# Transposing V by crossbar DMA instead of on TensorE in a two-block attention backward kernel

## The chip, the cores and the metric

The kernel runs on one core of one Trainium2 chip. The metric is the device time of one execution in microseconds (us). Engines are named as in the profile: PE (TensorE matmul), PEld (TensorE weight load), DVE (VectorE), ACT (ScalarE), POOL (GpSimd), SP (SyncE, which issues most transfers).

## The reference

Two independent attention blocks A and B, forward and all gradients. Each has 8 batches of 96 queries, 32 heads of width 128, 512 cached keys and values per head and batch, and a model width of 640.

```python
def _A_ref(x, k_cache, v_cache, wq, wo):          # B is the same
    q = (x @ wq) -> [B, H, Sq, Dh]
    scores = einsum("bhqd,bhkd->bhqk", q, k_cache) * Dh ** -0.5
    p = softmax(scores)
    o = einsum("bhqk,bhkd->bhqd", p, v_cache)
    return o -> [B, Sq, H*Dh] @ wo
# outputs: concat(a, b) and the gradients of x, k_cache, v_cache, wq, wo of both blocks
```

The backward pass needs dP = dO · Vᵀ, so V is used in both orientations: as stored (keys on partitions) for the output, and transposed (Dh on partitions) for dP. K is used transposed for the scores and as stored for dQ.

## The kernel before

The kernel is a software pipeline over 512 (head, batch) pairs. One pair enters per "tick"; its stages s1 to s8 run in the ticks after it, so that each tick holds one stage of each of several pairs, plus "filler" work per head (projections, weight gradients) that is spread over the eight ticks of a head.

```python
OFF = dict(ld=0, s1=2, s2=3, s3=3, s4=4, s5=5, s6=6, s7=7, s8=8)   # tick of each stage

def bank(shape, dt, name):            # all PSUM tiles share 8 banks
    return ps.tile(shape, dt, name=name, tag="bank")

def c_ld(h, b):                       # loads, one batch per transfer
    K_sb = kvp.tile([128, KC, 128], BF16, name="K_sb", bufs=11)
    V_sb = kvp.tile([128, KC, 128], BF16, name="V_sb", bufs=8)
    nc.sync.dma_start(K_sb[:], kc[b, h]...)
    nc.sync.dma_start(V_sb[:], vc[b, h]...)

def c_s1(h, b):                       # K and V transposed on PE, one eviction on DVE
    kvT_ps = bank([128, 2 * Sk], BF16, "kvT_ps")
    for c in range(KC):
        nc.tensor.transpose(kvT_ps[:, c*128:(c+1)*128], st["K_sb"][:, c, :], ident[:])
    for c in range(KC):
        nc.tensor.transpose(kvT_ps[:, Sk + c*128: ...], st["V_sb"][:, c, :], ident[:])
    KVT = wk.tile([128, 2 * Sk], BF16, name="KVT", bufs=5)
    nc.vector.tensor_copy(KVT[:], kvT_ps[:])

def c_s2a(h, b):                      # scores on PE, minus their maximum on DVE
    S_ps = bank([Sq, Sk], F32, "S_ps")
    nc.tensor.matmul(S_ps[:], QT_h[:, tok], KT)
    nc.vector.tensor_reduce(negm[:], S_ps[:], axis=AX.X, op=ALU.max, negate=True)

def c_s2b(h, b):                      # exp on ACT: reads S_ps for the last time
    nc.scalar.activation(E_sb[:], S_ps[:], ACT.Exp, bias=negm[:], accum_out=rowsum[:])

def c_s6(h, b):                       # dP and the row term, then dS on DVE
    nc.tensor.matmul(dP_ps[:], dOT_h[:, tok], VT)
    nc.tensor.matmul(dl_ps[:], prod[:], ones[:, 0:1])
    nc.vector.scalar_tensor_tensor(dS_sb[:], dP_ps[:], dl_ps[:, 0:1], P_sb[:], ...)
# ... (s3 to s5, s7, s8, the fillers and the set-up are cut)
```

## Time and profile before

| | before |
|---|---|
| time, median of 3 (lowest to highest) | 1850.45 us (1850.15 to 1851.11) |
| PE, DVE, ACT, POOL busy | 98%, 82%, 78%, 42% |
| chain that ended last | PE 95% |
| DMA, SyncE queue and GpSimd queue | 46.2% and 10.7% of the 16 engines |

The engine line of the page of before (busy us, share of the span, instructions), its chain of waits and its two busy DMA queues:

```profile
PE 1818.4 (98%) x26595; PEld 1571.4 (85%) x26744; DVE 1518.6 (82%) x3309; ACT 1434.4 (78%) x4041; POOL 777.9 (42%) x1378
...
q1 hardware_dynamic: 296480, 270.53, 46.2%
q0 software_dynamic: 19872, 60.32, 10.7%
...
PE 95%; POOL 2%; issue 1%; DVE 1%; DMA 1%; ACT 0%; POOLq 0%; SPq 0%; ACTq 0%
```

PE is the limit: 95% of the chain is PE, and the next engine, DVE, is busy for 82% (PEld is the loading of weights for PE itself).

The timeline of PE before (start, duration of the group, engine, line, operation):

```profile
1000.65 0.39 PE L243 MATMUL kvT_ps<-ident,K_sb 128*128 128x128 bf16 x4
1000.87 0.39 PE L245 MATMUL kvT_ps<-ident,V_sb 128*128 128x128 bf16 x4
1001.09 0.33 PE L370 MATMUL dq_dst_ps<-dST_sb,K_sb 128*128 128x96 bf16 x4
```

The group of four V transposes is on record as 0.39 us long, but the next group starts 0.22 us after it: matmuls overlap, and what one costs is the distance to the start of the next, about 56 ns here.

The same stretch by engine, in the windows view (busy us of PE, PEld, DVE, ACT, POOL; granted clock; DMA share; GB/s):

```profile
1000.00:1025.00 25.00, 24.89 (x382) 21.36 (x381) 22.10 (x49) 21.98 (x65) 11.46 (x22) 1.00 0.65 201
```

The timeline of before around one batch's scores, all engines, other lines left out:

```profile
1002.99 0.38 PE L259 MATMUL S_ps<-KVT,QT_h 128*96 128x512 bf16 x1
...
1003.45 0.68 DVE L159 COPY Qnat_h<-n_ps 96x1024 bf16<-96x1024 bf16 x1
1004.04 0.68 DVE L261 TENSOR_REDUCE negm<-S_ps 96x1 f32<-96x512 f32 x1
...
1004.81 0.68 ACT L271 ACTIVATE E_sb<-S_ps,negm 96x512 bf16<-96x512 f32 x1 [0.98 <-DVE negm L261]
1005.40 0.19 ACT L271 ACTIVATION_READ_ACCUMULATOR E_sb<-S_ps,negm 96x1 f32 x1
...
1005.62 0.16 PE L354 MATMUL dl_ps<-ones,prod 128*96 128x1 bf16 x1
1005.65 0.22 PE L445 MATMUL dwq_ps<-dQnat,x_nat 128*128 128x128 bf16 x1
```

The maximum (negm) runs on DVE after a 0.68 us copy that is in line before it; exp on ACT waits for it and is through 2.6 us after the scores began. The filler matmul at 1005.65 follows dl_ps without a gap.

### The profile page before, as it was taken

Reading aid. Unit: us, or ns where it says so; the run is one execution under the profiler, and the core shown is the slowest. Engines: PE = TensorE matmul, PEld = TensorE weight load, DVE = VectorE, ACT = ScalarE, POOL = GpSimd, SP = SyncE. Lnnn points to the kernel's source line nnn. Section 1 sums busy time; section 2 is a strip of 40 time slices with the busy share of each in tenths; the row PEclk is TensorE's granted clock in tenths of the full one; section 3 lists DMA queues with packets and bytes.
Section 4 is the critical chain, followed back from the end, with each engine's and each line's share of the span. In section 5 each row is a group of like instructions: output and inputs, shape, how many; then the busy total and the mean of one; then the engine's idle time right before and its main releaser. Section 6 shows DMA issues by size and latency. Waiting matters only on the chain.

```text
span 1848.8 us, 69797 instructions
## 1 busy us (share of the span) xinstructions
PE 1818.4 (98%) x26595; PEld 1571.4 (85%) x26744; DVE 1518.6 (82%) x3309; ACT 1434.4 (78%) x4041; POOL 777.9 (42%) x1378
## 2 busy tenths in 40 slices
PE   6999999999999999999999999999999999999998
PEld 5888888888888888888888888888888888888887
DVE  5888867888788887888878887678887888878885
ACT  4888877888668886788767888788876788767882
POOL 4444433444334443345455444334433444333435
PEclk9999999999999999999999999999999999999999
DMA  7666654666546655566575665456655566555652
GB/s 229 196 193 202 192 162 149 199 195 193 164 148 194 201 183 165 159 191 205 186 229 173 196 194 184 160 167 198 192 175 164 171 196 199 159 165 176 201 168 84
DMA packets 316688, 335.32 MB, mean 181 GB/s; under 512 B 38368, under 2 KB 302048, under 8 KB 316352
## 3 DMA queue, kind: packets, MB, share of 16 engines
q1 hardware_dynamic: 296480, 270.53, 46.2%
q0 software_dynamic: 19872, 60.32, 10.7%
q8 instruction: 210, 3.44, 0.8%
q14 instruction: 126, 1.03, 0.2%
HBM read 171.57 MB, written 159.12 MB: 179 GB/s over the span
## 4 chain that ended last, share of the span: by engine, by line
PE 95%; POOL 2%; issue 1%; DVE 1%; DMA 1%; ACT 0%; POOLq 0%; SPq 0%; ACTq 0%
PE q_ps L210 11%; PE o_ps L480 10%; PE dV_ps L330 6%; PE kvT_ps L243 6%; PE kvT_ps L245 6%; PE dK_ps L394 6%; PE dP_ps L352 6%; PE S_ps L259 6%; PE dwq_ps L445 6%; PE dwo_ps L425 5%; PE optp_ps L313 5%; PE dq_dst_ps L377 5%; PE optp_ps L306 5%; PE dq_dst_ps L370 5%; PE n_ps L225 3%; PE nat_ps L410 2%
## 5 line engine op out<-in xcount | busy, mean ns | idle before, releaser
L290 POOL TENSOR_SCALAR P_sb<-E_sb,rinv 96x512 bf16<-96x512 bf16 x512 | 354.2, 692 | 780.5 <-DVE rinv L281 775.2
L271 ACT ACTIVATE E_sb<-S_ps,negm 96x512 bf16<-96x512 f32 x512 | 349.1, 682 | 291.2 <-DVE negm L261 288.1
L356 DVE SCALAR_TENSOR_TENSOR dS_sb<-dP_ps,dl_ps,P_sb 96x512 bf16<-96x512 f32 x512 | 383.3, 749 | 108.1 <-PE dl_ps L354 103.1
L247 DVE COPY KVT<-kvT_ps 128x1024 bf16<-128x1024 bf16 x512 | 350.0, 684 | 70.7 <-PE kvT_ps L245 69.0
L261 DVE TENSOR_REDUCE negm<-S_ps 96x1 f32<-96x512 f32 x512 | 347.6, 679 | 35.8 <-PE S_ps L259 30.1
L332 ACT ACTIVATE dV_sb<-dV_ps 128x512 bf16<-128x512 f32 x512 | 313.3, 612 | 0.0
L396 ACT ACTIVATE dK_sb<-dK_ps 128x512 bf16<-128x512 f32 x512 | 300.5, 587 | 15.7 <-PE dK_ps L394 12.9
L319 ACT ACTIVATE PT_sb<-optp_ps 128x384 bf16<-128x384 bf16 x512 | 253.4, 495 | 0.0
L245 PE MATMUL kvT_ps<-ident,V_sb 128*128 128x128 bf16 x2048 | 198.0, 219 | 0.0
L394 PE MATMUL dK_ps<-Qnat_h,dS_sb 96*128 96x128 bf16 x2048 | 197.9, 219 | 0.0
L243 PE MATMUL kvT_ps<-ident,K_sb 128*128 128x128 bf16 x2048 | 197.9, 219 | 0.0
L330 PE MATMUL dV_ps<-dOnat_h,P_sb 96*128 96x128 bf16 x2048 | 197.9, 219 | 0.0
L259 PE MATMUL S_ps<-KVT,QT_h 128*96 128x512 bf16 x512 | 193.8, 379 | 2.2 <-DVE KVT L247 1.9
L352 PE MATMUL dP_ps<-KVT,dOT_h 128*96 128x512 bf16 x512 | 195.2, 381 | 0.0
L342 POOL TENSOR_TENSOR prod<-OT_h,dOT_h 128x96 bf16<-128x96 bf16 x512 | 186.2, 364 | 19.4 <-ACT OT_h L316 14.4
L243 PEld LDWEIGHTS <-K_sb 128*128 128x128 bf16 x2048 | 147.3, 98 | 36.9 <-issue 1.9
L379 DVE COPY dST_sb<-dq_dst_ps 128x384 bf16<-128x384 bf16 x512 | 175.4, 343 | 1.8 <-PE dq_dst_ps L377 0.8
L313 PE MATMUL optp_ps<-ident,P_sb 96*128 96x96 bf16 x2048 | 171.6, 205 | 2.3 <-POOL P_sb L290 2.0
L377 PE MATMUL dq_dst_ps<-ident,dS_sb 96*128 96x96 bf16 x2048 | 172.1, 206 | 0.5 <-DVE dS_sb L356 0.4
L306 PE MATMUL optp_ps<-PT_sb,V_sb 128*128 128x96 bf16 x2048 | 172.1, 206 | 0.0
L370 PE MATMUL dq_dst_ps<-dST_sb,K_sb 128*128 128x96 bf16 x2048 | 170.7, 206 | 0.0
L445 PE MATMUL dwq_ps<-dQnat,x_nat 128*128 128x128 bf16 x1920 | 143.2, 219 | 0.0
(84 smaller groups left out, 3949.8 us busy)
## 6 DMA issues: line engine op xcount, KB each, us to landing
out_dram<-dV_sb SPq DMA_DIRECT2D x512, 128.0 KB, 2.0
out_dram<-dK_sb SPq DMA_DIRECT2D x512, 128.0 KB, 2.3
K_sb<-in_A_k_cache_dram SPq DMA_DIRECT2D x256, 128.0 KB, 2.4
V_sb<-in_A_v_cache_dram SPq DMA_DIRECT2D x256, 128.0 KB, 2.5
K_sb<-in_B_k_cache_dram SPq DMA_DIRECT2D x256, 128.0 KB, 2.4
V_sb<-in_B_v_cache_dram SPq DMA_DIRECT2D x256, 128.0 KB, 2.5
out_dram<-dwq_sb POOLq DMA_DIRECT2D x64, 160.0 KB, 3.0
out_dram<-dwo_sb POOLq DMA_DIRECT2D x64, 160.0 KB, 2.7
```

The costliest lines, as they stand in the source:

```text
L243: nc.tensor.transpose(kvT_ps[:, c * 128:(c + 1) * 128], st["K_sb"][:, c, :], ident[:])
L245: nc.tensor.transpose(kvT_ps[:, Sk + c * 128:Sk + (c + 1) * 128], st["V_sb"][:, c, :], ident[:])
L247: nc.vector.tensor_copy(KVT[:], kvT_ps[:])
L259: nc.tensor.matmul(S_ps[:], hs["QT_h"][:, tok], st["KT"], start=True, stop=True)
L261: nc.vector.tensor_reduce(negm[:], S_ps[:], axis=AX.X, op=ALU.max, negate=True)
L271: nc.scalar.activation(E_sb[:], st["S_ps"][:], ACT.Exp, bias=st["negm"][:], scale=1.0, accum_out=rowsum[:])
L290: nc.gpsimd.tensor_scalar(P_sb[:], st["E_sb"][:], st["rinv"][:], 0.0, op0=ALU.mult, op1=ALU.add)
L330: nc.tensor.matmul(dV_ps[:, c * 128:(c + 1) * 128], P_sb[:, c * 128:(c + 1) * 128], hs["dOnat_h"][:, b * 128:(b + 1) * 128], start=True, s ...
L332: nc.scalar.activation(dV_sb[:], dV_ps[:], ACT.Identity, scale=1.0)
L352: nc.tensor.matmul(dP_ps[:], hs["dOT_h"][:, tok], st["VT"], start=True, stop=True)
L356: nc.vector.scalar_tensor_tensor(dS_sb[:], dP_ps[:], dl_ps[:, 0:1], st["P_sb"][:], op0=ALU.subtract, op1=ALU.mult)
L394: nc.tensor.matmul(dK_ps[:, c * 128:(c + 1) * 128], dS_sb[:, c * 128:(c + 1) * 128], hs["Qnat_h"][:, b * 128:(b + 1) * 128], start=True, s ...
```

## The change

The intent: PE has no time to spare and DMA has, so the four V transposes per pair leave PE, and a crossbar transfer from SBUF to SBUF makes VT. DVE then evicts half as many columns. Loads and crossbar transfers handle two batches each, to halve their number.

```diff
-OFF = dict(ld=0, s1=2, ...)
+OFF = dict(ld=-1, vt=1, s1=2, ...)
     def c_ld(h, b):
-            K_sb = kvp.tile([128, KC, 128], BF16, name="K_sb", bufs=11)
-            V_sb = kvp.tile([128, KC, 128], BF16, name="V_sb", bufs=8)
-            nc.sync.dma_start(K_sb[:], kc[b, h]...)
-            nc.sync.dma_start(V_sb[:], vc[b, h]...)
+            K_sb = kvp.tile([128, 2, KC, 128], BF16, name="K_sb", bufs=7)
+            V_sb = kvp.tile([128, 2, KC, 128], BF16, name="V_sb", bufs=5)
+            nc.sync.dma_start(V_sb[:], vc[b:b + 2, h]...)
+            nc.sync.dma_start(K_sb[:], kc[b:b + 2, h]...)
+    def c_vt(h, b):
+            VT = kvp.tile([128, 2 * KC, 128], BF16, name="VT", bufs=4)
+            nc.sync.dma_start_transpose(VT[:], V_sb[:].rearrange("p a c d -> p (a c d)"))
     def c_s1(h, b):
-            kvT_ps = bank([128, 2 * Sk], BF16, "kvT_ps")
+            kT_ps = bank([128, Sk], BF16, "kT_ps")
             # four transposes of K, as before
-            # four transposes of V
-            KVT = wk.tile([128, 2 * Sk], BF16, name="KVT", bufs=5)
-            nc.vector.tensor_copy(KVT[:], kvT_ps[:])
+            KT = wk.tile([128, Sk], BF16, name="KT", bufs=3)
+            nc.vector.tensor_copy(KT[:], kT_ps[:])
# ... c_ld and c_vt are called for even b only
```

More of the change, by code (lines that the diff above doesn't have):

```diff
@@ L43 @@
 SL_SETUP = 96
-OFF = dict(ld=0, s1=2, s2=3, s3=3, s4=4, s5=5, s6=6, s7=7, s8=8)
+OFF = dict(ld=-1, vt=1, s1=2, s2=3, s3=3, s4=4, s5=5, s6=6, s7=7, s8=8)
 HK = dict(pA=-5, pB=-3, pC0=[-2, 0], pC1=[-1, 0], pD1=1, pD0=2, qA0=13, qA1=17, qB=[20, 17], qD=[(18, 0, 2), (19, 2, 5)])
@@ L230, in f @@
         def f():
-            K_sb = kvp.tile([128, KC, 128], BF16, name="K_sb", bufs=11)
-            V_sb = kvp.tile([128, KC, 128], BF16, name="V_sb", bufs=8)
-            nc.sync.dma_start(K_sb[:], kc[b, h].rearrange("(p c) d -> p c d", c=KC))
-            nc.sync.dma_start(V_sb[:], vc[b, h].rearrange("(p c) d -> p c d", c=KC))
-            CS[(blk, h, b)] = dict(K_sb=K_sb, V_sb=V_sb)
+            K_sb = kvp.tile([128, 2, KC, 128], BF16, name="K_sb", bufs=7)
+            V_sb = kvp.tile([128, 2, KC, 128], BF16, name="V_sb", bufs=5)
+            nc.sync.dma_start(V_sb[:], vc[b:b + 2, h].rearrange("b (p c) d -> p b c d", c=KC))
+            nc.sync.dma_start(K_sb[:], kc[b:b + 2, h].rearrange("b (p c) d -> p b c d", c=KC))
+            for i in range(2):
+                CS[(blk, h, b + i)] = dict(K_sb=K_sb[:, i], V_sb=V_sb[:, i], V2=V_sb)
+        return f
+    def c_vt(h, b):
+        def f():
+            VT = kvp.tile([128, 2 * KC, 128], BF16, name="VT", bufs=4)
+            nc.sync.dma_start_transpose(VT[:], CS[(blk, h, b)]["V2"][:].rearrange("p a c d -> p (a c d)"))
+            for i in range(2):
+                CS[(blk, h, b + i)]["VT"] = VT[:, i * KC:(i + 1) * KC].rearrange("p c k -> p (c k)")
         return f
@@ L240, in f @@
             st = CS[(blk, h, b)]
-            kvT_ps = bank([128, 2 * Sk], BF16, "kvT_ps")
+            kT_ps = bank([128, Sk], BF16, "kT_ps")
             for c in range(KC):
-                nc.tensor.transpose(kvT_ps[:, c * 128:(c + 1) * 128], st["K_sb"][:, c, :], ident[:])
-            for c in range(KC):
-                nc.tensor.transpose(kvT_ps[:, Sk + c * 128:Sk + (c + 1) * 128], st["V_sb"][:, c, :], ident[:])
-            KVT = wk.tile([128, 2 * Sk], BF16, name="KVT", bufs=5)
-            nc.vector.tensor_copy(KVT[:], kvT_ps[:])
-            st["KT"] = KVT[:, 0:Sk]
-            st["VT"] = KVT[:, Sk:2 * Sk]
+                nc.tensor.transpose(kT_ps[:, c * 128:(c + 1) * 128], st["K_sb"][:, c, :], ident[:])
+            KT = wk.tile([128, Sk], BF16, name="KT", bufs=3)
+            nc.vector.tensor_copy(KT[:], kT_ps[:])
+            st["KT"] = KT[:]
         return f
@@ L511, in build_block @@
                 ct = c0t + b
-                em.add(ct + OFF["ld"], SLOTS["LOAD"], c_ld(h, b))
+                if b % 2 == 0:
+                    em.add(ct + OFF["ld"], SLOTS["LOAD"], c_ld(h, b))
+                    em.add(ct + OFF["vt"], SLOTS["LOAD"] + 1, c_vt(h, b))
                 em.add(ct + OFF["s1"], SLOTS["S1"], c_s1(h, b))
```

## The prediction

> **What bounds the kernel now.** TensorE. The page's engine table gives PE 98% busy, DVE 82%, ACT 78%, POOL 42%; the chain that ended last is 95% PE; the clock is 0.999. In the body the windows show PE 24.89 of every 25 us, and the list of waits gives PE about 5 us of waiting besides 12 us for the first input. One batch of one head takes about 3.1 us in dense stretches. DMA is not short: 46% of the 16 engines for the SyncE queue, 11% for the GpSimd queue, 0.63 in the dense windows. SyncE issues a plain transfer in 0.34 us and waits some 1,300 us in all.
>
> **What is removed.** The 4 V transposes per batch. Their duration (219 ns) is latency; what they cost is the spacing. In the timeline the next group starts 0.22 us after the V group (1000.87 to 1001.09), as in the chain ("kvT_ps x4, 0.22"). 512 x 0.225 = 115 us, all on the critical path: floor 1850 - 115 = 1735 us. DVE evicts 512 columns rather than 1024: 684 ns now; from the 384-, 640- and 768-column copies (343, 478, 544 ns) I estimate 410 ns, so DVE gives back about 140 us, off the path.
>
> **What is added.** 256 crossbar transfers of 256 KB. The trace has no such transfer. The Trainium skill ("DMA: Bandwidth & Descriptors", Latency and other measured facts) gives 261 GB/s for a non-contiguous transpose and 350 to 400 for a contiguous one; no run here shows it yet. Estimate from that page: 1.0 us each at 261 GB/s, 257 us of all 16 engines, 15% of the new span. DMA in dense windows goes from 0.63 to about 0.68 by the shorter tick plus 0.17: about 0.85. Busy, not full.
>
> **What moves.** Loads become 256 x 2 of 256 KB, the same bytes; SyncE issues 512 loads fewer and 256 transposes more, each holding SyncE longer than 0.34 us. In program order V lands two ticks (about 6 us; a load lands in 2.4 us) before its transpose, and VT is used five ticks (about 14 us) after: latency is hidden. Stores queue behind a transpose in SyncE, but dV_sb and dK_sb have three buffers.
>
> **What becomes next.** In a dense tick, ACT is 21.74/8 = 2.72 us, DVE 2.76 - 0.27 = 2.49 us, PE 3.11 - 0.22 = 2.89 us. PE stays first, but ACT is then at 94% there, in a chain (scores, DVE maximum, ACT exp, POOL scale, PE) with little slack. I allow 15 us of new PE idle time.
>
> **Prediction: 1750 us, 80% range 1728 to 1845.** Chances: faster by over 2% 0.76, within 2% 0.12, slower by over 2% 0.12.
>
> **What would show each step.** PE instructions fall by 2048, PE still 96% or more busy; K's transposes still 0.22 us apart. The eviction about 0.41 us, DVE about 1,380 us in all, ACT unchanged at about 1,434. DMA share up to 0.75 on average, transposes landing in 2 to 5 us. PE waits for VT or K_sb near zero; new PE idleness is on P_sb (POOL) or a bank that ACT holds.
>
> **What would make it wrong.** (1) The crossbar runs much below the page's rate: at a third of it the transfers would want about 45% of DMA, with 68% already taken; loads and stores fall behind and PE waits for V or K. This is the main risk, behind the range's upper end. (2) A transpose holds SyncE for several us: dK_sb and dV_sb stores go out late, ACT waits for those buffers, then PE. (3) ACT at 94% costs more than 15 us. Better than the floor is unlikely: nothing else leaves PE.

## The result and the profile after

The changed kernel takes 1766.29 us (median of 4 runs, 1763.59 to 1768.97). The ratio to before is 0.9545, 95% interval 0.9531 to 0.9558. (Ratios here are the mean time of one kernel's runs over that of the other's of the same rounds, so not quite the ratio of the medians.) Two of the four runs took 1763.6 us at a granted clock of 1.000 and two 1768.9 us at 0.997 and 0.998, so differences of 5 us between kernels need care. The profiled run is one of the first pair.

The engine line and the busy queues of the page of after:

```profile
PE 1727.7 (98%) x24696; PEld 1467.1 (83%) x24696; DVE 1407.1 (80%) x3309; ACT 1426.4 (81%) x4041; POOL 775.8 (44%) x1378
...
q1 hardware_dynamic: 558624, 337.64, 80.0%
q0 software_dynamic: 19872, 60.32, 12.3%
```

PE's weight loads fall by exactly 2048 (some matmul records of before are missing, so its matmul count falls by less), DVE by 112 us. The SyncE queue's share of DMA goes from 46% to 80%. (The page's chain of waits broke off near the end in this trace and is not used.)

The crossbar transfers in the DMA view (count, median us to landing), from the tile view how long SyncE was held by one (ns, min/median/max), and the new eviction in the groups:

```profile
VT<-V_sb SPq DMA_TRANSPOSE x256, 4.6
```

```profile
L242 SPq DMA_TRANSPOSE VT<-V_sb x256: 1231/1306/3567, 13.9 to 1706.1; - x128
```

```profile
L254 DVE COPY KT<-kT_ps 128x512 bf16<-128x512 bf16 x512 | 212.6, 415 | 44.5 <-PE kT_ps L252 44.3
```

PE, where the V group was, and the same window by engine:

```profile
1001.31 0.39 PE L252 MATMUL kT_ps<-ident,K_sb 128*128 128x128 bf16 x4
1001.53 0.33 PE L376 MATMUL dq_dst_ps<-dST_sb,K_sb 128*128 128x96 bf16 x4
```

```profile
1000.00:1025.00 25.00, 24.81 (x372) 20.96 (x371) 21.62 (x50) 23.01 (x67) 12.19 (x22) 1.00 1.10 277
```

ACT is now at 92% of this dense window, and the packets' times add up to 1.10 of the 16 DMA engines' time.

**What is missing.** I summed, from the start times in the trace, the distance from each matmul to the next one, by the group that the first belongs to. (The fillers q_ps and dwo_ps and the scores S_ps are added up, because 85 records of the first and 64 of the second are missing from some traces, that of before among them, and their time then falls to a neighbour; the sum does not suffer.)

| spacing on PE, us | before | after |
|---|---|---|
| V transposes | 116.1 | 0 |
| dl_ps | 16.2 | 39.8 |
| K transposes | 114.3 | 117.2 |
| q_ps + dwo_ps + S_ps | 422.2 | 422.3 |
| all others together | 1168.4 | 1170.9 |
| first to last matmul | 1837.2 | 1750.2 |

The V transposes were worth 116.1 us, as predicted, but only 87.0 arrived: 29.1 us came back as new gaps on PE, 23.6 of them behind dl_ps. In 103 ticks (47 before a dwq_ps filler, 56 before a q_ps filler) the next matmul starts 0.17 to 0.28 us after dl_ps, mostly 0.26, instead of 0.03. The list of waits shows none of this (its PE entries besides the first loads sum to 6.4 us), because a gap of 0.25 us is mostly hidden under the modelled 0.16 us of dl_ps itself and the ends of the matmuls before it. In 94 of these ticks (47 before each filler) it starts 50 to 52 ns after ACT has ended ACTIVATION_READ_ACCUMULATOR, the last step of exp, which reads the row sums; so it waits for exp. The timeline of after at the place shown of before:

```profile
1003.43 0.38 PE L265 MATMUL S_ps<-KT,QT_h 128*96 128x512 bf16 x1
...
1003.90 0.68 DVE L159 COPY Qnat_h<-n_ps 96x1024 bf16<-96x1024 bf16 x1
1004.50 0.68 DVE L267 TENSOR_REDUCE negm<-S_ps 96x1 f32<-96x512 f32 x1
...
1005.27 0.68 ACT L277 ACTIVATE E_sb<-S_ps,negm 96x512 bf16<-96x512 f32 x1 [0.78 <-DVE negm L267]
...
1005.84 0.17 PE L360 MATMUL dl_ps<-ones,prod 128*96 128x1 bf16 x1
1005.86 0.19 ACT L277 ACTIVATION_READ_ACCUMULATOR E_sb<-S_ps,negm 96x1 f32 x1
1006.10 0.22 PE L451 MATMUL dwq_ps<-dQnat,x_nat 128*128 128x128 bf16 x1
```

From the start of the scores to the end of exp and of the reading of its row sums (ACTIVATION_READ_ACCUMULATOR) it takes 2.62 us (1006.05 - 1003.43), as before (1005.59 - 1002.99 = 2.60). But PE comes round to dl_ps 2.41 us after the scores, not 2.63 us, and its next matmul starts only when exp is through. The trace does not name PSUM banks, but the compiled program does: the changed kernel puts the filler in all 94 ticks into the bank that the scores had, and lets it wait for ACT's semaphore.

**Theory A:** the 29 us are waits for banks, given back by the chain scores, maximum on DVE, exp on ACT, which did not get shorter with the tick. **Theory B, the rival:** they come from the crossbar transfers, which fill DMA and hold SyncE. Within A it was open whether ACT (92% busy here) or DVE is the slow member, or the number of banks.

### The profile page after: what moved, and what is told of

The parts are those of the page before. It is cut to its first block, busy times and chain, and to the rows that moved or that the text cites. A ratio compares the mean times of both kernels' runs of the same rounds, so it can differ in the third digit from the quotient of the medians.

```text
span 1761.8 us, 65690 instructions
## 1 busy us (share of the span) xinstructions
PE 1727.7 (98%) x24696; PEld 1467.1 (83%) x24696; DVE 1407.1 (80%) x3309; ACT 1426.4 (81%) x4041; POOL 775.8 (44%) x1378
## 5 line engine op out<-in xcount | busy, mean ns | idle before, releaser
L254 DVE COPY KT<-kT_ps 128x512 bf16<-128x512 bf16 x512 | 212.6, 415 | 44.5 <-PE kT_ps L252 44.3
L252 PE MATMUL kT_ps<-ident,K_sb 128*128 128x128 bf16 x2048 | 197.9, 219 | 0.0
L265 PE MATMUL S_ps<-KT,QT_h 128*96 128x512 bf16 x512 | 193.8, 378 | 1.7 <-DVE KT L254 1.5
L358 PE MATMUL dP_ps<-VT,dOT_h 128*96 128x512 bf16 x512 | 195.2, 381 | 0.0
L431 PE MATMUL dwo_ps<-g_nat,Onat 128*128 128x128 bf16 (+1 forms) x768 | 140.5, 299 | 0.1
```

The costliest lines, as they stand in the source:

```text
L252: nc.tensor.transpose(kT_ps[:, c * 128:(c + 1) * 128], st["K_sb"][:, c, :], ident[:])
L254: nc.vector.tensor_copy(KT[:], kT_ps[:])
L358: nc.tensor.matmul(dP_ps[:], hs["dOT_h"][:, tok], st["VT"], start=True, stop=True)
```

## The experiments

Twelve kernels ran, all derived from the changed kernel unless said otherwise. Times are medians; the ratio is to before.

### e1_no_vt: no transposition of V at all

```diff
-            nc.sync.dma_start_transpose(VT[:], V_sb[:]...)
-            CS[...]["VT"] = VT[:, i * KC:(i + 1) * KC]...
+            CS[...]["VT"] = V_sb[:, i].rearrange("p c d -> p (c d)")   # wrong on purpose
```

> The changed kernel without any transpose of V: dP reads V untransposed (dK, dQ and what follows from them are wrong on purpose); the order of instructions on PE, DVE and ACT is unchanged. Theory A (the 29 us of PE spacing beyond the floor are waits for a PSUM bank held until DVE's maximum and ACT's exp of the same scores are done): 1760 to 1770 us, the gap after dl_ps stays near 40 us in sum. Theory B (they come from the crossbar transfers: DMA share 93%, SyncE held 1.3 us each): 1735 to 1743 us.

Measured: 1764.93 us, ratio 0.9536 (0.9523 to 0.9549), the same as with the transfers. The same window of its trace, with a DMA share of 0.68 in place of 1.10:

```profile
1000.00:1025.00 25.00, 24.71 (x373) 20.99 (x372) 21.52 (x52) 23.04 (x68) 11.89 (x22) 1.00 0.68 204
```

The spacing behind dl_ps is 40.2 us, again with 56 and 47 long gaps. Theory B falls: in this kernel the 256 crossbar transfers cost nothing that these runs could show (1764.93 us without them, 1766.29 with them).

### e2_pe_back: V's transposes also back on PE, unread

```diff
-            kT_ps = bank([128, Sk], BF16, "kT_ps")
+            kT_ps = bank([128, 2 * Sk], BF16, "kT_ps")
+            for c in range(KC):
+                nc.tensor.transpose(kT_ps[:, Sk + c*128: ...], st["V_sb"][:, c, :], ident[:])
-            nc.vector.tensor_copy(KT[:], kT_ps[:])
+            nc.vector.tensor_copy(KT[:], kT_ps[:, 0:Sk])
```

> The changed kernel with the four V transposes per batch put back on PE into the unused half of the bank, read by nobody; the crossbar transfers stay and DVE still evicts 512 columns. Theory A: PE's 115 us come back and the bank waits vanish with the longer tick: 1846 to 1856 us, the same as before. Theory B: the transfers cost their 29 us here too: 1870 to 1885 us.

Measured: 1850.64 us, ratio 0.9999 (0.9985 to 1.0013). With PE's work back the whole gain is gone, although DVE is 102 us lighter than before (1416.3 us in its page) and the transfers run. The spacing behind dl_ps is 15.7 us, as before (in the slowest of its five runs, 1856.5 us, which was the one profiled). So PE's work alone makes the gain, and the waits appear only with the shorter tick.

### e3_dve_back: DVE's eviction doubled

```diff
-            KT = wk.tile([128, Sk], BF16, name="KT", bufs=3)
-            nc.vector.tensor_copy(KT[:], kT_ps[:])
+            KT = wk.tile([128, 2, Sk], BF16, name="KT", bufs=3)
+            nc.vector.tensor_copy(KT[:], kT_ps[:].unsqueeze(1).to_broadcast([128, 2, Sk]))
# to make room, the set-up pool has 4 buffers in place of 6
```

> The changed kernel with DVE's eviction of K doubled (512 columns written twice, 1024 as before, about 0.7 us in place of 0.415 us, some 140 us in all); PE and DMA unchanged. Theory A: DVE lies in the chain that gives back the bank, so its saving was on the path after all: 1775 to 1800 us, with longer waits after dl_ps. Theory B, and the prediction's word that DVE's saving is off the path: 1762 to 1770 us.

Measured: 1778.8 us, ratio 0.9611 (0.9598 to 0.9624): 12.5 us slower than the change. DVE's time is back to 1517.9 us. So DVE's saving was not off the path. The loss grows evenly over the run, so the smaller set-up pool does not explain it. The waits are not where I had said: the gaps behind dl_ps are shorter (29.7 us), and 16 us stand before the scores instead (spacing of dwq_ps 123.1 us against 107.0). There PE waits for KT, the very copy that was doubled, and not for a bank (its list of waits, which counts the longer ones only: total us, times, longest us):

```profile
PE S_ps L265 <- DVE KT L254: 11.0, 43, 1.8
```

This run therefore shows that DVE's time is on the path, but not that the maximum is. Waits move as soon as the timing moves; only their sum says something.

### e4_dl_bank: one bank allocation per tick less

```diff
-            kT_ps = bank([128, Sk], BF16, "kT_ps")
+            kT_ps = bank([128, 2 * Sk], BF16, "kT_ps"); KTB[tick] = kT_ps
-            dl_ps = bank([Sq, 1], F32, "dl_ps")
+            dl_ps = KTB.pop(tick)[0:Sq, Sk:Sk + 2].bitcast(F32)   # own bank for the last four
```

> The changed kernel with the 96x1 result dl_ps written into the unused half of the K bank in place of a bank of its own: one of eight bank allocations per tick less, all else equal, results right. Theory A: the bank is there when PE comes to it: 1738 to 1756 us, the gap after dl_ps falls below 25 us. Theory B: 1762 to 1770 us.

Measured: 1762.05 us, ratio 0.9522 (0.9509 to 0.9535), results right. The gaps behind dl_ps are gone (17.1 us of spacing, and none of the 47 before dwq_ps is left), so they were waits for a bank. But the time hardly fell and missed the 1738 to 1756 us of Theory A: dP_ps rose to 123.9 us (dl_ps now waits until DVE has read K's half of the same bank) and dq_dst_ps from 178.2 to 183.2. The number of banks was where PE waited, not why the chain was late.

### e5_spread: two long DVE copies moved

```diff
-            em.add(c0t + HK["pD0"], SL_HEAD, pD(h, 0))            # Qnat_h, 1024 columns
+            em.add(c0t + HK["pD0"], SL_HEAD, pD(h, 0, 0, 4))      # 512 columns
+            em.add(c0t + HK["pD0"] + 2, SL_HEAD, pD(h, 0, 4, 8))  # 512 columns
-HK = dict(... qA0=13 ...)
+HK = dict(... qA0=14 ...)                                        # Onat one tick later
```

> The changed kernel with two of DVE's long evictions moved: the Qnat_h copy (677 ns, which runs just ahead of the maximum in the ticks where PE then waited 0.25 us) is cut into two of 512 columns two ticks apart, and the Onat copy comes one tick later than the wqT_h copy; same work, results right. Theory A as refined by the traces (the bank of the scores comes back late because the maximum queues behind those copies on DVE): 1742 to 1757 us. If instead ACT's load (94% of a dense tick) is the limit whatever DVE's order: 1760 to 1770 us.

Measured: 1760.1 us, ratio 0.951 (0.9496 to 0.9524), results right. This misses the first expectation by 3 us and stands at the lower end of the second: a small gain, whose interval does not overlap the change's. dl_ps falls to 23.4 us, but dwq_ps rises to 116.2. Of the kernels whose arithmetic is unchanged it has the lowest median, though its interval overlaps that of e4_dl_bank.

### e6_loads: the kernel before with the new loads only

```diff
-OFF = dict(ld=0, ...)      # K_sb, V_sb per batch, 11 and 8 buffers
+OFF = dict(ld=-1, ...)     # K_sb, V_sb per two batches, 7 and 5 buffers; V on PE as before
```

> The kernel before with only the loads changed (two batches per transfer, issued one tick earlier, the new buffer counts), all transposes on PE. Every theory in which PE's work decides: 1848 to 1853 us. If the larger loads had a share in the gain: below 1845 us.

Measured: 1851.35 us, ratio 1.0004 (0.9989 to 1.0019). The larger loads have no share in the gain.

### e7_k_too: K by the crossbar as well

```diff
+            KT = kvp.tile([128, 2 * KC, 128], BF16, name="KT", bufs=3)
+            nc.sync.dma_start_transpose(KT[:], K_sb[:]...)
-            # the four transposes of K on PE and their eviction on DVE
# the set-up pool has 4 buffers in place of 6 here too
```

> The changed kernel with K transposed by the crossbar as well (256 more transfers; PE loses 2048 more transposes, DVE its K eviction, one bank allocation per tick less). If DMA and SyncE still have room: PE's floor is 1737 - 115 = 1622 us, ACT's 1426 us of work at 96% of a dense tick gives about 1660 to 1700 us. If the crossbar traffic does not fit (DMA share 0.93 plus about 0.35 by the measured time of V's packets, SyncE about 5 us of every 5.6): 1720 to 1850 us, with PE waiting on KT, and transposes landing in over 8 us.

Measured: 1925.6 us, ratio 1.0421: slower than before, by more than I had allowed for, at a granted clock of 0.966 to 0.973. The reason is not the one I named either: PE waits only 6.0 us for KT, and the transposes land in 4.6 and 4.9 us (medians), not in over 8. Its engine line, its queue, and the longest new waits of ACT and PE (total us, times, longest us):

```profile
PE 1694.2 (88%) x22499; PEld 1397.9 (73%) x22648; DVE 1249.1 (65%) x2797; ACT 1416.5 (74%) x4041; POOL 778.2 (41%) x1378
...
q1 hardware_dynamic: 828960, 404.78, 95.1%
```

```profile
ACT dK_sb L400 <- DMA out_dram<-dK_sb: 177.3, 122, 5.2
...
PE S_ps L263 <- ACT dK_sb L400: 141.4, 93, 5.3
```

SyncE's timeline shows why the dK stores are late (us that each held SyncE):

```profile
998.00 6.14 SPq L246 DMA_TRANSPOSE VT<-V_sb  x1
1004.24 0.52 SPq L337 DMA_DIRECT2D out_dram<-dV_sb  x1
1004.85 2.63 SPq L242 DMA_TRANSPOSE KT<-K_sb  x1
1007.57 0.53 SPq L233 DMA_DIRECT2D V_sb<-in_B_v_cache_dram  x1
1008.19 0.42 SPq L401 DMA_DIRECT2D out_dram<-dK_sb  x1
```

A transposing transfer here holds SyncE for up to 6 us (median 1.4), the stores queue behind it, ACT runs out of dK_sb buffers, and PE waits for the bank that ACT has not read. The prediction feared this chain for V. With V alone it does not occur (ACT waits 0.5 us for stores); with K too it does. Whether the full DMA engines or SyncE's own issue work come first was not separated, nor what share of the loss is the lower clock's.

### e8_micro: the crossbar transfer by itself

The kernel's body is replaced by 24 loads of V pairs, 24 transposing transfers back to back from the last pair to the first, and 24 stores; the outputs are wrong.

```diff
+        for i in range(24): nc.sync.dma_start(V[i][:], ...)
+        for i in reversed(range(24)): nc.sync.dma_start_transpose(VT[i][:], V[i][:]...)
+        for i in ...: nc.sync.dma_start(dv[...], VT[i][...])
```

> The transfer by itself (results missing on purpose): 24 V pairs are loaded, then 24 crossbar transposes[...] are issued back to back from SyncE with nothing else in flight, then stored. If the transfer's own cost is the 18 ns that most of its 256-byte packets took: about 1.2 us of the 16 engines each, spaced by SyncE's 1.3 us. If the mean of 34 ns is its own cost and not queueing: 2.2 us each, spaced by 2.2 us.

Measured, in its timeline, in the tile view (how long each held SyncE, ns min/median/max) and in the window in which only these transfers run (POOL busy, clock, DMA share, GB/s):

```profile
20.33 33.01 SPq L586 DMA_TRANSPOSE VT<-V  x24
```

```profile
L586 SPq DMA_TRANSPOSE VT<-V x24: 1267/1332/1346, 20.3 to 52.0; - x24
```

```profile
22.00:52.00 30.00, 0.00 (x0) 1.00 1.00 190
```

One takes 33.01 / 24 = 1.38 us at 190 GB/s, and the times of its packets add up to 1.36 us of all 16 engines: near the first expectation, not the second, and above the 1.0 us of the prediction. But SyncE is held for nearly all of each 1.38 us, so it is not separated whether SyncE's issue or the DMA engines set this pace. In the changed kernel the packets of one add up to more: (80.0% of 1761.8 - 46.2% of 1848.8) / 256 = 2.17 us, and the sum over its 256-byte packets is the same. Most of these took 18 ns and the slowest hundredth over 580 ns, where alone the slowest hundredth took 59 ns or more: the rest comes with the other traffic.

### e9_balance and e10_balance_before: evictions redistributed

```diff
-EV = dict(pB0="act", pB1="dve", pC00="act", pC01="act", pC10="act", pC11="dve", pD0="dve", pD1="dve", qA0="dve", qA1="dve", qB0="act", qB1="act", qD="dve", gU="act")
+EV = dict(pB0="dve", pB1="dve", pC00="dve", pC01="act", pC10="dve", pC11="dve", pD0="dve", pD1="dve", qA0="act", qA1="act", qB0="dve", qB1="dve", qD="act", gU="act")
```

> The changed kernel with only the table changed that says which of ACT and DVE evicts each head's projections and gradients, so that in each of a head's eight ticks both stay near or under PE's tick (PE, DMA and buffers unchanged, results right). By my sums DVE now has 1.2 us of extra copies in two ticks running and ACT 0.6 to 0.7 us in four running, which leaves the scores' maximum and exp late. If this local overload is the cause of PE's 29 us: 1738 to 1752 us, stalls after dl_ps below 8 us. If the order within a tick or the number of banks is the limit whatever the load: 1758 to 1770 us.

> The same table in the kernel before. There PE hardly waits (spacing within a few us of its floor), so nothing is to be had: 1846 to 1852 us. If the table were good by itself and not because of the shorter tick: below 1843 us.

Measured: e9 1765.67 us, ratio 0.9538 (0.9524 to 0.9552), no change. e10 1851.58 us, ratio 1.0003 (0.9986 to 1.002), no change either. e9 says little: it did not do what it set out to. ACT takes 0.83 to 0.85 us for a copy that takes DVE 0.55 us, so ACT's total only went from 1426 to 1416 us, and DVE's rose from 1407 to 1452 us. Its waits moved too (dl_ps 24.7 us, dwq_ps 117.7). It left open whether ACT or DVE is the slow one.

### e11_act_less: ACT relieved, nothing else

```diff
-            nc.scalar.activation(dV_sb[:], dV_ps[:], ACT.Identity, scale=1.0)
+            nc.scalar.activation(dV_sb[:, 0:256], dV_ps[:, 0:256], ACT.Identity, scale=1.0)   # wrong on purpose
# and the store writes only these columns
```

> The changed kernel with ACT's dV eviction and its store cut to half their columns (dV is incomplete on purpose): about 210 ns of ACT less per batch, some 110 us in all; the instructions and their order on PE, DVE and GpSimd are exactly those of the changed kernel. The first balancing run did not relieve ACT (1416 us in place of 1426, since ACT takes 0.84 us for a copy that takes DVE 0.55). If ACT, in order and at 92 to 94% of a dense tick, is what PE waits for: 1737 to 1748 us, spacing after dl_ps below 22 us, dK evictions starting 0.2 us sooner. If it is DVE alone: 1758 to 1768 us.

Measured: 1767.95 us, ratio 0.9552 (0.9539 to 0.9565), with 100 us less on ACT:

```profile
PE 1721.7 (97%) x24547; PEld 1468.2 (83%) x24696; DVE 1407.3 (80%) x3309; ACT 1326.4 (75%) x4041; POOL 775.8 (44%) x1378
```

dl_ps keeps 40.3 us with the same 56 and 47 gaps, and ACT starts to evict dK exactly as late as in the change (391 ns after PE's last dK matmul in both, 203 ns before the change; means over the trace). The 5 us by which the profiled run is longer are lost before the first 32 pairs are through (its clock was 0.997); after that it keeps the pace of the change to 0.1 us. ACT's other work is not what makes the chain late. A shorter exp, which is in the chain itself, was not tried.

### e12_max_half: the maximum over half the scores

```diff
-                nc.vector.tensor_reduce(negm[:], S_ps[:], axis=AX.X, op=ALU.max, negate=True)
+                nc.vector.tensor_reduce(negm[:], S_ps[:, 0:256], axis=AX.X, op=ALU.max, negate=True)
```

> The changed kernel with DVE's maximum taken over 256 of the 512 scores (any shift gives the same softmax as long as exp stays in range, so the results should still be right here): about 0.27 us of DVE less per batch, some 135 us in all, in the chain scores, maximum, exp; about a tenth of DVE's instructions also change places. If DVE's share in that chain is what gives the banks back late: 1740 to 1755 us, the mirror image of the doubled eviction, which cost 12 us. If ACT alone: 1758 to 1768 us.

Measured: 1740.4 us, ratio 0.9407 (0.9394 to 0.942), results right on this input. The maximum in the groups of after and of this kernel:

```profile
L267 DVE TENSOR_REDUCE negm<-S_ps 96x1 f32<-96x512 f32 x512 | 347.4, 679 | 38.1 <-PE S_ps L265 32.7
```

```profile
L267 DVE TENSOR_REDUCE negm<-S_ps 96x1 f32<-96x256 f32 x512 | 211.1, 412 | 39.6 <-PE S_ps L265 34.1
```

dl_ps is down to 14.6 us, with no gap of over 0.15 us before the two fillers in place of 103, and the sum from first to last matmul is 1724.5 us, 3.4 above the floor of 1837.2 - 116.1 = 1721.1. From the start of the scores to the end of exp (without the reading of the row sums) it takes 2.15 us on average before, 2.13 in the change and in e11, and 1.82 here; and ACT's evictions of dK start 203 ns after PE's last dK matmul again, as before the change. This kernel is not offered as a better version: a score that the maximum leaves out could overflow exp on another input. About a tenth of DVE's instructions also stand in another order than in the change, so its gain is that of a shorter maximum together with that order.

## Why the prediction was right or wrong, point by point

- **PE is the limit and V's transposes cost 115 us of it: right.** They took 116.1 us of spacing, and e2_pe_back takes the gain away by putting just that work back.
- **The time of 1750 us, range 1728 to 1845: right, with the gain smaller than forecast**, 84 us in place of 100. Part of the 16 us between is the granted clock: two of the runs took 1763.6 us at clock 1.000.
- **"I allow 15 us of new PE idle time": the term that was too small.** It measured 29.1 us. The chain that the prediction names is the right one as far as exp, and so is "a bank that ACT holds"; for P_sb (POOL) PE waits only 2.6 us.
- **Its reason, "ACT is then at 94% there": wrong.** ACT did reach 92% and PE did wait for ACT, but e11_act_less gave ACT 100 us back and changed nothing. The late member is DVE: in all 94 ticks exp begins 91 to 95 ns after the end of the maximum, with ACT idle before it (on average 0.79 us before dwq_ps fillers, 0.12 us before q_ps), while the maximum begins directly behind a long copy on DVE (Qnat_h in 47, Onat in 46, wqT_h in one). Everything behind exp on ACT is late with it.
- **"DVE gives back about 140 us, off the path": wrong in its second half.** The eviction's own time fell by 137 us (350.0 to 212.6 in the groups), DVE's busy time as a whole by 112. Giving DVE the eviction back costs 12.5 us, in waits for KT (e3_dve_back), and taking 135 us more from the maximum gains 26 us (e12_max_half). An engine at 80% was on the path by its latency: its work comes in order, and each tick needs KT and the maximum from it in time.
- **Eviction 0.41 us, ACT unchanged, landing in 2 to 5 us: right** (0.415 us, 1426 us, 4.6 us).
- **"DMA share up to 0.75 on average": wrong.** It is 0.93. The mis-sized term is the 1.0 us of all engines per transfer: alone it is 1.38 us, and 2.17 us among the other traffic. It did no harm, as e1_no_vt shows; that a miss of this size was free was luck, and e7_k_too shows that it need not be.
- **"No waits for VT or K_sb; latency is hidden": right.** The list of waits has none.
- **A transpose holding SyncE: harmless at 1.3 us each for V, decisive when K was added** (e7_k_too).

What stays open: of the 29.1 us, the cause is followed one by one only in the 94 ticks, which hold 21.9 us of them. How the gain of e12 divides between the shorter chain, less DVE work in all and its other order was not separated; less DVE work elsewhere was not tried.

## What to carry to other kernels

When work leaves the limiting engine, every chain whose length does not shrink with the tick comes closer to its deadline; look for the one with the least slack before and after (here scores, maximum, exp: 2.6 us against a tick of about 3), and not only for the engine with the highest share. Measure the limiting engine by the distance between starts, since short waits hide under modelled durations, and judge an attempt by the sum of these distances, since waits wander. A DMA share near 1 can be free, and the next step in the same direction can still cost 9%: try both.

## What the Trainium skill lacked or had wrong

- "DMA: Bandwidth & Descriptors", Latency and other measured facts, gives 261 GB/s for a non-contiguous transposing DMA and 350 to 400 for a contiguous one. This case shows 190 GB/s for 256 KB transfers from SBUF to SBUF with nothing else in flight (1.38 us each), and the measurement decides for transfers issued one after the other by SyncE, which may set this pace itself.
- "Advanced Engine Details and Errata", X-Bar Transpose (TRN2), says that transposing DMAs are as fast as regular ones. In the changed kernel most 256-byte packets of the transpose took 18 ns and most 1024-byte packets of plain loads and stores 46 ns: per byte, the transpose takes about 1.6 times as long (72 ns per 1024 bytes).
- "DMA: Bandwidth & Descriptors" gives no measured time on this chip for which a transposing transfer holds its issuing engine (only cycles for "previous generations", in a table on a later chip). Here one of 256 KB holds SyncE for 1.31 us (median), against 0.39 us for a plain load of the same size, and up to 6.1 us in e7_k_too.
- "TensorE: Matmul & The Clock Gate", Back-to-back issue gap, gives about 81 ns per matmul of 128 columns for a stream of weight loads and matmuls. The transposes here, each with its own weight load, follow each other at 56 ns.
- The same page (Architectural detail) says that ACT and DVE are strictly first in, first out. The traces agree: the maximum stands behind a 0.68 us copy. What it lacks is the consequence seen here, that an engine at 80% can set the pace by what stands before its one urgent instruction.
